# V rows in one tile, X blocks in pairs, and late K weights, in the prologue of a two-part kernel

## The chip, the cores and the metric

One core of one Trainium2 chip. The metric is the device time of one execution in microseconds (us), lower is better. The kernel before took 2195.29 us in the median of four runs (2187.41 to 2197.44). Ratios are computed as the mean time of one kernel's runs over the mean of the other's runs of the same rounds, so they are not quite the ratio of the medians quoted beside them.

## The reference

Two independent computations share the program; their outputs lie side by side.

```python
# A: a long convolution (here done by two-stage DFTs), S = 2048, D = 1024
kv = shifted(k, shift_k) * v
y  = irfft(rfft(pad(kv)) * rfft(pad(ssm_k)))[:S] + kv * ssm_D
a  = q * y
# B: 64 segments of 32 tokens, each attends to itself and to a memory of 8 rows (1024 wide, 32 heads of 128)
for s in range(64):
    h = concat([mem, x[32*s : 32*s+32]])          # 40 rows
    q, k, v = h @ Wq, h @ Wk, h @ Wv
    o = softmax(mask(q k^T * scale)) v @ Wo
    mem = o[:8]; outs.append(o[8:])
out = concat([a, b], axis=-1)
```

The memory makes the segments of B a chain. Each needs all four weight matrices, which do not fit in SBUF together. So the kernel keeps 43 of 64 chunks of weights (512 KB each) in SBUF, and two more from the first segment on; the other 19 it streams in each segment from a copy in DRAM, `WS`, through a ring of six tiles. What does not depend on the memory (projections of the last eight tokens of each segment, transposed X) is computed ahead, in a prologue, where A runs too.

## The kernel before

The parts that the change touches. `slot16` hands out two tiles of 16 KB per partition in turn, `pair` two tiles of 4 KB in turn; `group` loads one group of eight weight chunks and copies the streamed ones to `WS`. `VBD` is the buffer in DRAM for the V rows, `REC` that for transposed X and the other projections.

```python
def slot16(shape, dt, name):
    turns["stage"] ^= 1
    return base.tile(shape, dt, tag=f"stage{turns['stage']}", name=name)
def pair():
    turns["pair"] ^= 1
    return base.tile([128, 2048], BF, tag=f"wring{2 + turns['pair']}", name="pair")

# transposed X blocks, one every third unit of A's work: X and its transposed copy share a tile
def x_load(b):
    both = pair()
    nc.sync.dma_start(both[:, 0:1024], x[b * 128:(b + 1) * 128, :])
    loaded.append(both)
def x_block(b):
    both = loaded.pop(0)
    X_sb = both[:, 0:1024]
    ...                                     # eight transposes on TensorE into PSUM tile tp
    xt = both[:, 1024:2048].rearrange("p (s k t) -> p s k t", s=4, k=8)
    nc.vector.tensor_copy(xt, tp[:].rearrange(...))
    nc.gpsimd.dma_start(REC[:, 4 * b:4 * b + 4, 0:256], xt.rearrange("p s k t -> p s (k t)"))

# weights that stay, but come late; then the V projection and its stores
def place_late(n, tile_of):                 # n chunks of `late` into a tile, by GpSimd's queue
    ...
with tc.issue_after(copied[-4].ins):        # behind one of the last copies to WS
    place_late(4, stage_home)               # four K chunks into a 16 KB tile
    for i in range(len(v_temp) - 2, n_more):
        place_late(1, lambda: more(i))
for _ in range(2):
    fetch()                                 # first two chunks of the ring
...                                         # six Wo chunks DRAM to DRAM into WS
for g in range(2):
    ws = wv[g]
    for tb in range(4):                     # four row blocks of 128
        vst = pair()[:].rearrange("p (c w) -> p c w", c=4)
        for c in range(4):
            ...                             # eight matmuls into ps
            evac(vst[:, c, :], ps[:])       # ScalarE twice, VectorE once, in turn
        for c in range(4):
            nc.sync.dma_start(VBD[16*tb:16*tb+16, :, c, :, g*128:(g+1)*128].rearrange("s t i e -> (s t) i e"),
                              vst[:, c, :].rearrange("p (i e) -> p i e", i=4))   # 128 KB in 256 B pieces
    if g == 0:
        place_late(4, stage_home)           # four Wo chunks into the other 16 KB tile
        for i in range(2):
            place_late(1, lambda: more(i))
```

## Time and profile before

| stretch of the span, us | what runs | full resource |
|---|---|---|
| 0 to 115 | A, first DFT stage | mixed |
| 115 to 293 | A, second stage, filled with B's projections and X blocks | TensorE |
| 293 to 369 | A, third stage, filled with the Q projection | DMA |
| 369 to 453 | V projection (256 matmuls of 128x512) | DMA, then TensorE |
| 453 to 2190 | 64 segments, some 27 us each | DMA |

The prediction below shows the lines themselves. Two marks separate the prologue from the loop: the first and the last V matmul, and the first output of the loop, which is the first issue of `out_dram<-Y`. In the timeline of GpSimd of the kernel before it reads (start, duration, engine, line, operation; in brackets the idle time before it and what ended it):

```profile
490.09 0.74 POOL L1033 DMA_DIRECT2D out_dram<-Y  x1 [7.73 <-ACT Y L1026]
```

### The profile page before, as it was taken

What the parts mean: (1) busy time and instruction counts of PE and PEld (TensorE: products, weight loads), DVE (VectorE), ACT (ScalarE), POOL (GpSimd) and SP (SyncE); (2) the same over time, 40 slices, a digit from 0 to 9 for tenths busy, and PEclk for the clock granted to TensorE, in tenths of its full rate; (3) what the DMA queues carried; (4) which work ended last, traced back from release to release, by engine and by line L of the source; (5) the groups of instructions that cost most, each with busy time, mean ns of one, the idle gap of its engine ahead of it and who ended that gap; (6) DMA issues with size and microseconds to landing.
All of it is one profiled execution on the core that took longest, in us unless ns stands there. A gap on an engine that the chain in (4) does not pass through costs nothing. (4 is left out here: it accounts for less than half of the span.)

```text
span 2190.4 us, 81498 instructions
## 1 busy us (share of the span) xinstructions
PE 1734.6 (79%) x35636; PEld 927.5 (42%) x35636; DVE 872.0 (40%) x2686; ACT 648.4 (30%) x1139; POOL 436.8 (20%) x1131
## 2 busy tenths in 40 slices
PE   4688888678878878888887887888878888888886
PEld 2232233234444444444444444444444444444444
DVE  9927752023333333333333333333333333333332
ACT  8935521122222222222222222222222222222221
POOL 4013422311111111111111111111111211111111
PEclk9899999889999999999999999999999999999999
DMA  9998879889999999999999999999999999999996
GB/s 324 340 341 295 267 274 391 277 293 383 388 379 392 393 356 385 392 391 395 392 387 385 393 391 391 394 395 374 396 393 374 388 383 384 389 394 392 394 389 263
DMA packets 262702, 804.66 MB, mean 367 GB/s; under 512 B 52332, under 2 KB 52364, under 8 KB 262343
## 3 DMA queue, kind: packets, MB, share of 16 engines
q1 hardware_dynamic: 230008, 725.84, 86.9%
q0 software_dynamic: 27120, 63.11, 8.4%
q10 hardware_dynamic: 5216, 10.49, 1.3%
q8 instruction: 279, 4.57, 0.8%
q14 instruction: 79, 0.65, 0.1%
HBM read 739.92 MB, written 62.39 MB: 366 GB/s over the span
## 5 line engine op out<-in xcount | busy, mean ns | idle before, releaser
L884 PEld LDWEIGHTS <-rec 128*32 128x32 bf16 x12351 | 324.2, 96 | 477.8 <-issue 259.1
L884 PE MATMUL acc<-wring,rec 128*32 128x512 bf16 (+1 forms) x3777 | 375.9, 386 | 141.6 <-DMA wring<-WS 126.4
L893 ACT CAST qkv_sb<-acc 128x512 bf16<-128x512 f32 x384 | 224.8, 585 | 660.8 <-PE acc L884 660.8
L970 PEld LDWEIGHTS <-OT 128*32 128x32 bf16 x8192 | 216.3, 96 | 178.2 <-issue 151.3
L970 PE MATMUL yacc<-wring,OT 128*32 128x256 bf16 x3072 | 153.9, 275 | 98.0 <-DMA wring<-WS 56.4
L884 PE MATMUL acc<-Wmid,rec 128*32 128x512 bf16 x3072 | 225.8, 383 | 0.0
L884 PE MATMUL acc<-Wres,rec 128*32 128x512 bf16 x2816 | 221.2, 380 | 0.0
L830 PEld LDWEIGHTS <-OTB 128*16 128x16 bf16 x4096 | 105.1, 90 | 105.5 <-issue 95.1
L956 ACT CAST OT<-OTp 128x512 bf16<-128x512 f32 x128 | 74.9, 585 | 242.9 <-PE OTp L948 242.9
L986 DVE COPY KT<-tps 128x512 bf16<-128x512 bf16 x64 | 27.2, 424 | 298.6 <-PE tps L899 298.6
L785 POOL DMA_DIRECT2D rec<-REC x64 | 37.5, 585 | 526.6 <-issue 277.2
L957 DVE CAST OTB<-OTp 128x128 bf16<-128x128 f32 x128 | 37.3, 291 | 262.1 <-ACT OT L956 262.1
L736 DVE TENSOR_SCALAR wring<-OTp 128x384 int32<-128x384 int32 x126 | 112.2, 890 | 58.4 <-PE acc L884 52.4
L884 PE MATMUL acc<-pw,rec 128*32 128x512 bf16 x1536 | 130.4, 382 | 0.0
L860 POOL COPY KT<-rec 128x128 bf16<-128x128 bf16 x128 | 38.6, 302 | 427.8 <-PE SB L908 421.9
L845 POOL DMA_DIRECT2D out_dram<-YB x128 | 73.0, 577 | 234.2 <-DVE YB L843 224.0
L914 DVE TENSOR_REDUCE mx<-SB 128x5 f32<-128x200 f32 x128 | 47.1, 368 | 181.4 <-PE SB L908 181.4
L830 PE MATMUL SB<-wring,OTB 128*16 128x256 bf16 x1488 | 78.2, 273 | 39.1 <-DVE SB L809 31.0
L899 PE MATMUL tps<-ident,qkv_sb 128*128 128x128 bf16 x1024 | 101.0, 221 | 8.0 <-ACT qkv_sb L893 0.2
L899 PEld LDWEIGHTS <-qkv_sb 128*128 128x128 bf16 x1024 | 62.6, 97 | 105.0 <-ACT qkv_sb L893 67.5
L970 PE MATMUL yacc<-Wlate,OT 128*32 128x256 bf16 x2048 | 93.4, 273 | 2.9 <-issue 2.7
L1026 ACT CAST Y<-yacc 128x256 bf16<-128x256 f32 x64 | 23.8, 372 | 242.8 <-PE yacc L970 238.9
(229 smaller groups left out, 2690.1 us busy)
## 6 DMA issues: line engine op xcount, KB each, us to landing
wring<-WS SPq DMA_DIRECT2D x1216, 512.0 KB, 7.4
rec<-REC POOLq DMA_DIRECT2D x64, 192.0 KB, 6.1
SK<-s_sb SPq DMA_DIRECT2D x16, 512.0 KB, 4.9
SU<-s_sb SPq DMA_DIRECT2D x16, 512.0 KB, 5.0
Kg<-SK SPq DMA_DIRECT2D x32, 256.0 KB, 4.5
Ug<-SU SPq DMA_DIRECT2D x32, 256.0 KB, 5.6
REC<-stage POOLq DMA_DIRECT2D x16, 512.0 KB, 9.7
zt<-SZ SPq DMA_DIRECT2D x16, 512.0 KB, 8.7
```

Source lines behind the costliest of these rows:

```text
L736: nc.vector.tensor_scalar(out=dst, in0=src, scalar1=0, scalar2=None, op0=ALU.bitwise_or)
L785: nc.gpsimd.dma_start(rec[:], REC[:, s, :])
L830: nc.tensor.matmul(self.acc[32 * dq:32 * dq + W, x - o:y - o], lhsT=self.OTB[:, c, 4 * g + i, :], rhs=r, start=first and not self.seeded, ...
L845: nc.gpsimd.dma_start(bass.AP(outb.tensor, outb.offset + (SEG * NB * self.b + NX) * 2048 + 256 * dq, [[2048 * SEG, NB], [2048, 8], [1, 256 ...
L860: nc.gpsimd.tensor_copy(KT[:, :, :, 32:40], KBs[:, 128 * g:128 * g + 128].rearrange("p (c i t) -> p i c t", c=4, i=4))
L884: nc.tensor.matmul(self.acc[32 * c:32 * c + 32, x - 512 * c:y - 512 * c], lhsT=hT[:, kc, :], rhs=r, start=(kc == 0 and x == 512 * c), stop ...
L893: nc.scalar.copy(sb[:], self.acc[:])
L899: nc.tensor.transpose(tp[:, i * 128:(i + 1) * 128], sb[:, i * 128:(i + 1) * 128], ident[:])
L914: nc.vector.tensor_reduce(out=mx[:], in_=S, op=ALU.max, axis=AX.X)
L956: nc.scalar.copy(OT[:], o_view[:, :, :, 0:32])
L957: nc.vector.tensor_copy(OTB[:, :, 4 * g:4 * g + 4, 8 * j:8 * j + 8], o_view[:, :, :, 32:40])
L970: nc.tensor.matmul(yacc[32 * dq:32 * dq + 32, x - o:y - o], lhsT=OT[:, c, i, :], rhs=r, start=(h == 0 and x == o), stop=(h == 31), tile_po ...
```

## The change

The intent, as I read it: V rows of group 0 should not wait for stores; an X load should not wait for a store of an older block's transposed copy; and late weights should not get in front of the V weights.

```diff
 def x_load(b):
-    both = pair()
-    nc.sync.dma_start(both[:, 0:1024], x[b * 128:(b + 1) * 128, :])
-    loaded.append(both)
+    t = base.tile([128, 2048], BF, tag="wring2", name="X_sb")
+    nc.sync.dma_start(t[:].rearrange("p (b d) -> p b d", b=2), x[b*128:(b+2)*128, :].rearrange("(b p) d -> p b d", b=2))
+    loaded[b], loaded[b + 1] = t[:, 0:1024], t[:, 1024:2048]
 def x_block(b):
-    both = loaded.pop(0)
-    X_sb = both[:, 0:1024]
+    X_sb = loaded.pop(b)
+    if b % 2 == 0:
+        t = base.tile([128, 2048], BF, tag="wring3", name="xt")
+        xts[b], xts[b + 1] = t[:, 0:1024], t[:, 1024:2048]
 ...                     # the load of a pair is issued after the second block of the pair before
-        with tc.issue_after(copied[-4].ins):
-            place_late(4, stage_home)
-            for i in range(len(v_temp) - 2, n_more):
-                place_late(1, lambda: more(i))
-        for _ in range(2):
-            fetch()
+        with tc.issue_after(copied[-1].ins):
+            for _ in range(2):
+                fetch()
+        late = late[4:11] + late[:4] + late[11:]          # K chunks behind seven Wo chunks
 ...
         for g in range(2):
+            if g == 0:
+                vsts = slot16([128, 4, 4, 512], BF, "vst")
             for tb in range(4):
-                vst = pair()[:].rearrange("p (c w) -> p c w", c=4)
+                vst = vsts[:, tb] if g == 0 else pair()[:].rearrange("p (c w) -> p c w", c=4)
 ...
             if g == 0:
-                place_late(4, stage_home)
-                for i in range(2):
-                    place_late(1, lambda: more(i))
+                with tc.issue_after(copied[-1].ins):
+                    place_late(4, stage_home)
+                    for i in [*range(len(v_temp) - 2, n_more), 0, 1]:
+                        place_late(1, lambda: more(i))
+                    place_late(4, stage_home)              # K, into the tile of group 0's V rows
```

More of the change, by code (lines that the diff above doesn't have):

```diff
@@ L545, in group @@
         return ws
-    loaded = []
+    loaded = {}
     def x_load(b):
-        both = pair()
-        nc.sync.dma_start(both[:, 0:1024], x[b * 128:(b + 1) * 128, :])
-        loaded.append(both)
+        t = base.tile([128, 2048], BF, tag="wring2", name="X_sb")
+        nc.sync.dma_start(t[:].rearrange("p (b d) -> p b d", b=2),
+                          x[b * 128:(b + 2) * 128, :].rearrange("(b p) d -> p b d", b=2))
+        loaded[b], loaded[b + 1] = t[:, 0:1024], t[:, 1024:2048]
     def x_block(b):
-        both = loaded.pop(0)
-        X_sb = both[:, 0:1024]
+        X_sb = loaded.pop(b)
+        if b % 2 == 0:
+            t = base.tile([128, 2048], BF, tag="wring3", name="xt")
+            xts[b], xts[b + 1] = t[:, 0:1024], t[:, 1024:2048]
         tp = ps0.tile([128, 1024], BF, tag="ps0", name="xt_ps")
@@ L559, in x_block @@
             nc.tensor.transpose(tp[:, kc * 128:(kc + 1) * 128], X_sb[:, kc * 128:(kc + 1) * 128], ident[:])
-        xt = both[:, 1024:2048].rearrange("p (s k t) -> p s k t", s=4, k=8)
+        xt = xts.pop(b).rearrange("p (s k t) -> p s k t", s=4, k=8)
         nc.vector.tensor_copy(xt, tp[:].rearrange("p (k j t) -> p j k t", k=8, j=4))
         nc.gpsimd.dma_start(REC[:, 4 * b:4 * b + 4, 0:256], xt.rearrange("p s k t -> p s (k t)"))
+    xts = {}
     flip = [0]
@@ L617, in fill @@
         units[0] += 1
+        if n == 0:
+            x_load(0)
         if n % 3 == 2 and blocks:
-            x_block(blocks.pop(0))
+            b = blocks.pop(0)
+            x_block(b)
+            if b % 2 and blocks:
+                x_load(b + 1)
         if n >= 34 or n % 3 != 2:
             next(rest, None)
-        if n % 3 == 0 and len(blocks) > len(loaded):
-            x_load(n_seg // 4 - len(blocks))
     run_a(pw, slot16, stage1_done, fill)
```

## The prediction

> **What bounds the kernel now.** I began with the granted clock (0.971, one core, a fast run), then the page's 40 slices and its chain. The chain that ended last is mostly DMA:
>
> ```profile
> DMA 14%; PE 5%; DVE 2%; issue 1%; ACT 0%; POOL 0%; SPq 0%; DVEq 0%; POOLq 0%; ACTq 0%
> DMA wring<-WS 14%; PE acc L884 2%; DVE wring L736 1%; PE yacc L970 1%; PE SB L830 1%; DMA out_dram<-YB 0%; PE tps L899 0%; ACT OT L956 0%; POOL out_dram L845 0%; PE OTp L944 0%; PE OTp L948 0%; DVE PT L935 0%; DVE OTB L957 0%; PE tps L791 0%; SPq L654 0%
> ```
>
> The 64 segments stream their weights from WS, 19 chunks of 512 KB each. From about 490 us on this loop is limited by the DMA engines, and the diff touches nothing in it. So the gain, if any, lies in the prologue, which I cut into stretches of one regime (busy time by engine, granted clock, DMA share and rate in each window; 1.00 DMA is all 16 engines at work):
>
> ```profile
> core 0: us, PE busy (x) PEld busy (x) DVE busy (x) ACT busy (x) POOL busy (x), PEclk, DMA share, GB/s
> 180.00:260.00 80.00, 77.01 (x426) 25.24 (x426) 67.69 (x118) 47.91 (x91) 35.51 (x34) 0.97 0.83 274
> 260.00:270.00 10.00, 4.27 (x18) 1.55 (x18) 3.08 (x5) 2.74 (x6) 3.64 (x5) 0.66 0.80 244
> 293.00:369.00 76.00, 64.09 (x284) 27.20 (x283) 28.10 (x32) 9.17 (x16) 21.42 (x33) 0.91 0.99 368
> 369.00:420.00 51.00, 27.10 (x117) 11.73 (x116) 3.46 (x5) 5.76 (x10) 15.02 (x20) 0.83 1.03 361
> 420.00:453.00 33.00, 33.00 (x147) 14.54 (x144) 3.73 (x6) 7.02 (x12) 6.36 (x12) 0.95 0.48 115
> 1000.00:2190.00 1190.00, 955.37 (x23529) 546.95 (x23517) 428.64 (x1543) 302.60 (x573) 213.01 (x668) 0.99 1.00 383
> ```
>
> To be seen: up to 293 us (stage 2 of the first half of the problem) TensorE is full, but for a hole at 260:270. From 293 the DMA is full. From 369 to 453 the V projection runs; in its first part TensorE is busy 27 of 51 us while the DMA is full, in its second part TensorE is full and the DMA half idle. That is two resources taking turns, which is where a reordering can gain. The waits of TensorE and of the two engines that evacuate PSUM, in the V part (total, times, longest):
>
> ```profile
> ACT pair L569 <- DMA VBD<-pair: 27.9, 2, 16.4
> PE vb_ps L694 <- ACT pair L569: 21.8, 2, 14.2
> DVE pair L571 <- DMA VBD<-pair: 18.0, 1, 18.0
> PE vb_ps L694 <- DMA Wres<-in_B_Wv_dram: 2.1, 1, 2.1
> ```
>
> V rows of group 0 fill two `pair` tiles in turn; the third and fourth row blocks wait until the stores of the first and second have landed in VBD. TensorE loses 7.6 us at 389 and 14.2 us at 405. The X blocks have a smaller loss of the same kind (TensorE in stage 2; then SyncE's queue, from 200 us on):
>
> ```profile
> PE xt_ps L559 <- DMA pair<-in_B_x_dram: 12.7, 2, 6.6
> SPq L551 <- DMA REC<-pair: 24.5, 7, 5.2
> ```
>
> A `pair` tile holds X and its transposed copy, so a new X load waits for the store of an older copy to REC, and SyncE's queue waits with it; then eight transposes, in order in TensorE's queue, wait for X (6.6 us to 180.1, 6.1 us to 265.7).
>
> **What the Trainium skill says.** (1) "DMA: Bandwidth & Descriptors", section "Queues, rings and completion order": each DMA engine takes turns between queues packet by packet. The trace agrees in direction: between 396 and 419 us only about four of the 128 KB VBD stores (256 B pieces, SyncE's queue) landed beside twelve or more 512 KB transfers of GpSimd's queue, with up to 21.1 us from issue to landing; once that queue had run dry, four landed within 1.4 us. (2) The same page, "Issuing engines are not separate DMA queues": a transfer moved to another place still needs the same 16 engines. So I keep a ledger of DMA work, not of queues. (3) "TensorE: Matmul & The Clock Gate", Part 1: after a few idle us the clock starts at half rate. Here too: the first matmuls after the 7.6 and 14.2 us waits come every 0.43 us, later ones every 0.216, at about 3 us a time. A removed wait gives that back too.
>
> **The change part by part.**
>
> *V rows of group 0 in one tile of 16 KB per partition.* All four row blocks get room of their own; the tile is the "stage" buffer whose last store (of the Q projection before) landed at 355.6, long before the first write at 373.6. So group 0 waits for no store. V needs 2 x 128 matmuls at 0.216 us = 55.3 us; it now runs 369.4 to 452.6 = 83.2. Of the surplus 27.9 us, 21.8 are the two waits, 2.1 the weights, and some 4 the slow clock after them. On TensorE alone the end could come at 424.7.
>
> *K weights behind Wo, ring prefetch later.* Before the last V weights, GpSimd's queue now issues two ring chunks and two K chunks (355.6 and 367); after the change they come later, and so do two more K chunks and one Wo chunk. That frees 4 x 1.35 us (512 KB at 390 GB/s) = 5 us of DMA ahead of the V weights: the 2.1 us wait should go. Bytes are the same. New dependency: the four K chunks go into the V tile, so they wait for all 16 stores of group 0, and the first segment wants them at once.
>
> *The DMA ledger.* From 369 to 453 the windows hold 1.03 x 51 + 0.48 x 33 = 68 us of full-time DMA work. At the highest share seen in 10 us windows there, 1.05, that takes 65 us: not before 434. Of TensorE's 28 us this leaves 28 - (434 - 425) = some 18. A second count by bytes: 361 GB/s x 51 us + 115 x 33 = 22 MB, of which the 32 VBD stores and four stage stores (6.3 MB) go in 256 B pieces, at the 290 GB/s of those four stores 22 us, and 15.9 MB at 400 GB/s 40 us: 62 us, an end at 431, a gain of 21. Stepping through by hand: GpSimd's queue is dry at about 416 to 419, group 0's stores land just after, K lands at about 428, and row blocks 2 and 3 of group 1 wait some 8 us for the stores of 0 and 1; V ends at about 432 to 435. I take **17 us**.
>
> *X in pairs.* Eight loads of 512 KB replace sixteen of 256 KB, each free to go once the transposes of the block before are done (three units, some 10 us, ahead of use), not after a store. The order of SyncE's instructions confirms that block 2's load moves ahead of weights it now follows. Of the 6.6 us I expect 3 to 4 back (issued about 5 us earlier, but twice as long), of the 6.1 us some 5: **8 us**. Stage 2 is TensorE's, so a hole there shifts all that follows. Transposes, copies and REC stores are unchanged in number and size.
>
> Sum: 17 + 8 = **25 us** of 2196.9.
>
> **The rivals.** *A. A new wait takes over*: group 0's stores queue up in front of group 1's, and K behind them. For it: SyncE's queue is in order and slow while GpSimd's is full. Against it: GpSimd's queue runs dry by about 419 and small stores then land at 0.45 us each. If K came only at 440, V's gain would fall to 12 and the sum to some 18 us: 2179. *B. The transfer is hidden*: stages after 293 are DMA-full, so earlier X helps nothing and V gains only what DMA idles. Against it for X: it removes a hole in which the DMA idled too (0.80), and the engines idle at 0.35 before 293. If X gave nothing: 2180. *C. TensorE is the only bound*: the shares above 1.0 under contention count waiting as work, and all 28 + 10 us come: 2159. *D. DVE becomes a wait*: the single transposed tile is rewritten only after two REC stores have landed (4 to 13 us each), and DVE would hold up stage 2; 2 to 4 us at the worst.
>
> **Range and chances.** Centre 2197 - 25 = **2172 us**. Low end: rival C, 2159 and a good run; high end: A and B together, 10 us gained, 2187. The runs before differ by 10 us among themselves (2187 to 2197), so I say **2157 to 2187**, 8 in 10. For 2% the gain would have to be 44 us; all prologue waits touched sum to 21.8 + 2.1 + 4 + 12.7 = 41 us. So faster by over 2%: **0.02**; within 2%: **0.97**; slower by over 2%: **0.01**, since bytes, matmuls and loop are the same.
>
> **What would show it.** Right: no wait of ACT or DVE on VBD in group 0; the last V matmul 20 to 28 us earlier than 452.6, of which some 8 already at the first V matmul; waits of the X transposes from 12.7 to about 4 us; DMA share above 0.9 up to the end of V; the loop still 27 us a segment ((2190.4 - 490.1) / 63). Wrong, if the first segment stalls on the K chunks in the V tile for more than a few us, if group 1's third row block waits over 15 us for VBD, if the DMA share still falls to 0.5 in V (then there was room for more, or a new wait), or if stage 2 ends no earlier.

## The result

The changed kernel took 2173.27 us in the median of four runs (2170.49 to 2175.60), for 2195.29 before; ratio 0.9906 with a 95% interval of 0.9878 to 0.9934. That is 20.6 us shorter by the ratio, and within 2%. The prediction said 2172, 2157 to 2187.

The chain that ended last is of the same make, the ring of weights. Its shares sum to 14% of the span (22% before), so it covers the end of the loop alone and says nothing of the prologue:

```profile
DMA 10%; PE 3%; DVE 1%; issue 0%; ACT 0%; POOL 0%; SPq 0%; POOLq 0%; DVEq 0%; ACTq 0%
```

The same windows as before (columns as above):

```profile
core 0: us, PE busy (x) PEld busy (x) DVE busy (x) ACT busy (x) POOL busy (x), PEclk, DMA share, GB/s
180.00:260.00 80.00, 74.72 (x422) 25.23 (x421) 66.95 (x117) 48.62 (x93) 35.02 (x33) 1.00 0.88 287
260.00:270.00 10.00, 9.03 (x49) 2.79 (x46) 8.45 (x16) 5.66 (x11) 7.09 (x8) 1.00 0.58 201
...
293.00:369.00 76.00, 63.84 (x279) 27.47 (x279) 27.61 (x31) 9.17 (x16) 21.29 (x31) 0.91 1.03 384
369.00:420.00 51.00, 40.81 (x187) 18.28 (x185) 5.54 (x8) 9.02 (x16) 17.26 (x26) 0.92 1.01 320
420.00:453.00 33.00, 22.36 (x192) 9.03 (x194) 4.40 (x12) 4.11 (x7) 5.25 (x16) 0.81 0.86 283
```

The hole at 260 to 270 us is gone (TensorE 9.0 us busy for 4.3). From 369 to 420 TensorE and the DMA are now busy together, 40.8 us for 27.1, and from 420 to 453 the DMA no longer runs half idle (0.86 for 0.48): V ends at 433.6, and the segments begin there. V now runs from 363.2 to 433.6, that is 70.4 us for 83.3.

The waits in the V part of the changed kernel (total, times, longest):

```profile
DVE pair L575 <- DMA VBD<-pair: 24.7, 2, 14.0
...
ACT pair L573 <- DMA VBD<-pair: 16.9, 2, 12.4
...
POOL Wlate L665 <- DMA VBD<-pair: 15.0, 1, 15.0
PE vb_ps L701 <- ACT pair L573: 10.2, 1, 10.2
```

Group 0's tile, `vst`, has no line that waits for a store. Group 1's `pair` tiles have: TensorE waits 10.2 us at 408, and 2.5 us later on. The third line is the new dependency: GpSimd's queue stood 15 us before it could load the K chunks (the profile names the tile of the last stores; by the program it is group 0's stores that are waited for). They were issued from 416.3 to 418.0 and landed from 422.0 to 426.2, before V ended.

The X blocks, from 150 us on:

```profile
PE xt_ps L562 <- DMA X_sb<-in_B_x_dram: 3.9, 1, 3.9
SPq L551 <- PE xt_ps L562: 10.3, 5, 3.1
DVE xt L564 <- DMA REC<-xt: 9.1, 3, 5.4
```

Transposes wait 3.9 us for X (12.7 before). SyncE's queue waits for TensorE, no longer for stores. VectorE has a new wait for the transposed tile's stores, 9.1 us, of which little reached TensorE: it waited 2.4 us for VectorE's `xt`, where before it had waited 2.1 us for the same copy. The first output of the loop comes 19.5 us earlier:

```profile
470.57 0.74 POOL L1042 DMA_DIRECT2D out_dram<-Y  x1 [7.75 <-ACT Y L1035]
```

### The profile page after: what moved, and what is told of

It is laid out like the page before. It is cut to its first block, busy times and chain, and to the rows that moved or that the text cites. A ratio compares the mean times of both kernels' runs of the same rounds, so it can differ in the third digit from the quotient of the medians.

```text
span 2173.7 us, 81452 instructions
## 1 busy us (share of the span) xinstructions
PE 1729.0 (80%) x35636; PEld 926.4 (43%) x35636; DVE 872.6 (40%) x2686; ACT 649.2 (30%) x1139; POOL 438.3 (20%) x1131
## 5 line engine op out<-in xcount | busy, mean ns | idle before, releaser
L979 PE MATMUL yacc<-Wlate,OT 128*32 128x256 bf16 x2048 | 104.5, 273 | 1.9 <-issue 1.0
L1035 ACT CAST Y<-yacc 128x256 bf16<-128x256 f32 x64 | 23.9, 373 | 239.7 <-PE yacc L979 230.2
```

The costliest lines, as they stand in the source:

```text
L979: nc.tensor.matmul(yacc[32 * dq:32 * dq + 32, x - o:y - o], lhsT=OT[:, c, i, :], rhs=r, start=(h == 0 and x == o), stop=(h == 31), tile_po ...
```

## The experiments

Theory: the gain is the sum of two independent parts. X in pairs shifts the end of stage 2; V rows in one tile let TensorE run beside the DMA; how much the latter gives is set by the DMA work that must be done anyway (the ledger). Rivals: the DMA hides the X part; TensorE alone decides V; the gain comes from the new order of late weights and ring chunks.

Twelve experiments ran, two of them the unedited kernels, each in five rounds, with runs of the kernel before among them. All gave the correct result but `big_pieces`. "V" is the first to last V matmul, "waits" are TensorE's in it, "loop" runs from the first to the last `out_dram<-Y`.

| kernel | median, us | before in its rounds | ratio (95%) | V, us | waits in V | first output | loop |
|---|---|---|---|---|---|---|---|
| before | 2195.29 | | | 369.4 to 452.7 | 23.9 | 490.1 | 1689.2 |
| changed | 2173.27 | 2195.29 | 0.9906 (0.9878 to 0.9934) | 363.2 to 433.6 | 12.7 | 470.6 | 1692.4 |
| x_only | 2186.43 | 2188.80 | 0.9987 (0.9973 to 1.0002) | 364.4 to 447.2 | 21.8 | 484.0 | 1693.0 |
| v_only | 2177.03 | 2188.80 | 0.9942 (0.9927 to 0.9957) | 368.4 to 437.7 | 11.6 | 475.0 | 1688.2 |
| k_first | 2173.68 | 2188.80 | 0.9922 (0.9898 to 0.9946) | 364.8 to 432.2 | 10.0 | 469.5 | 1693.8 |
| g1_own | 2168.36 | 2188.80 | 0.9911 (0.9891 to 0.9931) | 363.1 to 418.5 | 0 | 465.9 | 1700.5 |
| after_again | 2175.64 | 2190.76 | 0.9921 (0.9892 to 0.9949) | 359.3 to 428.9 | 11.8 | 465.8 | 1697.1 |
| before_again | 2188.48 | 2190.76 | 0.9979 (0.9949 to 1.0010) | 368.8 to 452.3 | 23.0 | 489.5 | 1691.9 |
| big_pieces | 2166.22 | 2190.76 | 0.9882 (0.9858 to 0.9906) | 362.4 to 424.6 | 5.1 | 460.2 | 1693.5 |
| whole_rows | 2167.51 | 2190.76 | 0.9894 (0.9870 to 0.9918) | 360.1 to 423.5 | 4.7 | 464.8 | 1698.3 |
| whole_rows_ring | 2168.54 | 2189.85 | 0.9891 (0.9862 to 0.9920) | 365.7 to 428.7 | 4.7 | 467.0 | 1690.8 |
| x_only_again | 2182.68 | 2189.85 | 0.9957 (0.9925 to 0.9990) | 362.7 to 444.4 | 22.1 | 482.5 | 1686.6 |
| v_only_again | 2179.30 | 2189.85 | 0.9949 (0.9916 to 0.9982) | 369.5 to 440.2 | 13.3 | 476.3 | 1691.9 |
| ring_early | 2169.11 | 2189.85 | 0.9900 (0.9871 to 0.9929) | 364.3 to 430.6 | 8.0 | 468.4 | 1693.8 |

One more mark can be taken from the table: from V's start to the first output. It leaves out what happens before V and in the loop, and the four kernels that were profiled twice repeat it within 0.9 us: 120.7 and 120.7 us for the kernel before, 119.6 and 119.8 for x_only, 106.6 and 106.8 for v_only, 107.4 and 106.5 for the changed kernel.

### x_only: the X part alone

The first half of the diff above (`x_load`, `x_block` and the point of the load), nothing of the V part.

> Only the X part of the change (pairs, transposed tiles of their own); V part as before. My theory: the holes in stage 2 shrink (waits of the X transposes from 12.7 to about 4 us), the first V matmul moves from 369.4 to about 363, the V part keeps its 83 us, and the whole is 6 us (4 to 8) shorter than before. Rival 'hidden': the DMA is full from 293 us on, so an earlier stage 2 is absorbed by slower stage 3 loads; first V matmul after 367, whole within 2 us of before.

TensorE's waits in the V part and for X, of x_only:

```profile
PE vb_ps L701 <- ACT pair L573: 21.8, 2, 12.2
PE xt_ps L562 <- DMA X_sb<-in_B_x_dram: 4.6, 1, 4.6
```

V starts at 364.4, 5.0 us earlier, its two waits of together 21.8 us stay, and the first output is 6.1 us earlier: the rival 'hidden' falls, as an earlier stage 2 goes straight through the DMA-full stretch. But the time gained was only 2.8 us, with an interval that includes 0, because this run's loop took some 4 us longer.

### v_only: the V part alone

The second half of the diff; X as before.

> Only the V part (group 0 in one tile, late loads and ring prefetch moved, K behind Wo); X as before. My theory (the ledger of DMA work): V part from 83 to about 70 us, with 10 to 13 us of waiting left in group 1, whole 13 us (10 to 16) shorter than before; with x_only it adds up to the whole change (20 to 22). Rival 'TensorE alone': V part near 56 us, whole 25 us or more shorter. Rival 'needs X': less than 6 us.

The same waits, of v_only:

```profile
PE vb_ps L694 <- ACT pair L569: 9.5, 1, 9.5
PE vb_ps L694 <- DVE pair L571: 2.1, 1, 2.1
PE xt_ps L559 <- DMA pair<-in_B_x_dram: 11.6, 2, 6.0
```

V takes 69.3 us, with 11.6 us of waits left, all in group 1; the time is 12.7 us shorter. Both are what the ledger expected and far from 'TensorE alone' (25 us or more). That expectation was written when the changed kernel's 70.4 us and 12.7 us of waits were known, so the numbers test that the V part alone brings them, not the ledger's size. The 2.1 us wait for the V weights does not appear.

### x_only_again and v_only_again: is the X part's loss in the loop real?

The same two kernels once more.

> x_only once more. In the first try its prologue was 6.1 us shorter (first loop output 484.0 for 490.1) but the time only 2.8 us (interval -0.4 to 5.9 us), as its loop took 1693 us for 1689. Theory 'loop scatter': first output within 2 us of 484, loop anywhere in 1687 to 1700, whole 4 to 7 us shorter than before. Rival 'X slows the loop': loop above 1692 again, whole 1 to 4 us shorter.

> v_only once more, the other half of that test. Theory 'loop scatter': first output within 2 us of 475.0, loop anywhere in 1687 to 1700, whole 13 to 16 us shorter than before. Rival 'only the X part lengthens the loop': loop 1686 to 1691 again.

The first outputs repeat (482.5 and 476.3); the loops do not: 1686.6 for x_only, the shortest of all, and 1691.9 for v_only. Both times missed what I had expected: 9.4 us shorter than before for 4 to 7, and 11.2 for 13 to 16. So 'X slows the loop' falls in the form that I had given it. Over the two tries x_only is 2.8 and 9.4 us shorter than before, mean 6.1, v_only 12.7 and 11.2, mean 12.0; together 18.1, for 20.6 and 17.3 (mean 19.0) of the whole change. Within this scatter the two parts add up. Not settled: ten profiles with the X part have loops of 1694 us in the mean, four without it 1690; single loops differ by 6 us in the same kernel, so I take no cause from that.

### after_again and before_again: the scatter

Both kernels unedited, among the others.

> The changed kernel, not edited, in the same rounds as the other three: 20 us (17 to 23) shorter than before. Its profile also shows how much the 64-segment loop differs from run to run: my theory is that first output of the loop comes within 2 us of 470.6 and that the loop from there to its last output (1692.4 us in the first profile) moves by up to 5 us without any cause in the change.

> The kernel before, not edited, as a null test: ratio 1.000 within 0.2%. First output of the loop within 2 us of 490.1; loop from there to the last output 1689.2 plus or minus 5 us. Rival 'the X part slows the loop' (x_only's loop took 1693.1, v_only's 1688.2): then before_again stays at 1688 to 1690 and after_again at 1692 to 1694.

The null test gave 0.9979 (interval to 1.001), just outside the 0.2% expected: five rounds can be off by 4 us or so. The changed kernel came out 17.3 us shorter by the ratio, within its expectation, but its first output at 465.8 was 4.8 us earlier than in the first profile, outside the 2 us I had given; stage 2 ended earlier (V from 359.3), and the loop took those 4.7 us longer. In this profile no wait of TensorE is put down to X, where the first one had a wait of 3.9 us. Of the ten profiles with the X part, seven have such a wait (3.9 to 5.2 us) and three have none (after_again, big_pieces and whole_rows, with V from 359.3, 362.4 and 360.1). Scatter in the prologue is thus larger than I believed, and a profile's single loop time says nothing at this level.

### k_first: the late weights in their old order

```diff
-        late = late[4:11] + late[:4] + late[11:]
```

> The changed kernel, but with the late weights in their old order: K into the other 16 KB tile first, Wo into the V tile last. My theory: the order of these loads is not what gained, because both wait behind the same DMA work and segment 0 starts after V either way; within 3 us of the changed kernel (20 to 22 us shorter than before). Rival 'K behind Wo matters': K first leaves the Wo chunks late for segment 0 or lengthens the wait of group 1, and 5 us or more of the gain go.

17.1 us shorter by the ratio, for 17.3 of after_again (in other rounds) and 20.6 of the first measurement; V's waits are 10.0 us and its first output 469.5. The order of K and Wo is not what gained: as shown for the changed kernel, K landed before V ended even when it came last.

### ring_early: the two ring chunks as early as before

```diff
-        with tc.issue_after(copied[-1].ins):
-            for _ in range(2):
-                fetch()
+        for _ in range(2):
+            fetch()
```

> The changed kernel with the two ring chunks loaded as early as before (ahead of the V copies). My theory (DMA work moved, not removed): the V weights arrive 2 to 3 us later, which costs at most 2 us in the first V rows; V ends within 2 us of the changed kernel's 428.9 to 433.6 and the time within 3 us of it (17 to 21 shorter than before). Rival 'the later prefetch was worth its 5 us of DMA': 4 us or more of the gain go.

21.9 us shorter, V ends at 430.6, first output 468.4; no wait for V weights showed. The later prefetch is not what gained either. k_first and ring_early each undo one move; from V's start to the first output they take 104.7 and 104.1 us, for 107.4 and 106.5 with the moves in. Undoing both, with the V tile kept, was not tried, nor can K go to its old place, which is now the V tile.

### g1_own: no V row waits for a store

As k_first, and group 1 gets the other 16 KB tile; its four Wo chunks come after V.

```diff
+        both = [slot16([128, 4, 4, 512], BF, "vst") for _ in range(2)]
         for g in range(2):
-                vst = vsts[:, tb] if g == 0 else pair()[:].rearrange("p (c w) -> p c w", c=4)
+                vst = both[g][:, tb]
 ...
-                    place_late(4, stage_home)      # after group 0
+        place_late(4, stage_home)                  # after V
```

> As k_first, but group 1's V rows get a 16 KB tile of their own too, so that no V row waits for a store to VBD; four Wo chunks then load only after V. My theory (ledger): TensorE's waits in V (12.7 us) vanish and V ends near 419, but the DMA was at a share of about 0.9 already, so the work left over delays segment 0; whole at most 6 us shorter than the changed kernel (20 to 27 shorter than before). Rival 'TensorE's chain': the whole wait is gained, 32 us or more shorter than before.

This is the clearest test of the ledger. V ran without a wait, 55.4 us for the 55.3 worked out in the prediction, and ended at 418.5, 15 us before the changed kernel. The first output came only 4.7 us earlier than its 470.6, and no earlier than after_again's 465.8. Against k_first, from which this edit starts, the way from V's start to the first output is 1.9 us shorter (102.8 for 104.7). The windows of g1_own, and the two longest waits of TensorE after V:

```profile
363.00:420.00 57.00, 55.72 (x259) 25.05 (x256) 8.04 (x13) 12.87 (x22) 18.32 (x28) 1.00 1.00 317
420.00:453.00 33.00, 16.25 (x198) 6.08 (x202) 5.00 (x19) 4.59 (x8) 7.34 (x18) 0.63 1.02 360
```

```profile
423.87 0.37 PE L799 MATMUL tps<-ident,Y 128*128 128x128 bf16 x2 [5.15 <-DMA Y<-in_B_mem_dram]
...
433.20 0.62 PE L892 MATMUL acc<-wring,rec 128*32 128x512 bf16 x4 [7.20 <-DMA wring<-WS]
```

The DMA is full (1.00 and 1.02) right through, and TensorE waits in segment 0 for a load instead of in V for a store. From the end of V to the first output it takes 47.4 us for 37.0 in the changed kernel: of the 15.1 us by which V ended earlier, 10.4 came back one stage later. (The two waits shown are 5.2 and 7.2 us; the changed kernel too has waits for ring chunks there, 4.1 and 2.3 us.) The edit itself also puts four chunks behind V, so this shows that the wait could not simply be removed with these tiles, and the full DMA (1.00 from 363 to 420) is, as I read it, the reason: the loads would have found no idle time ahead of V's end either. The time, 19.5 us shorter than before and just short of the 20 to 27 expected, cannot be told from the changed kernel's.

### big_pieces: the cost of 256 B pieces by itself

The same bytes in the same number of stores, but each partition writes 1 KB in one piece, to wrong places in `VBD`; the second half of the output is wrong.

```diff
-    VBD[16*tb:16*tb+16, :, c, :, g*128:(g+1)*128].rearrange("s t i e -> (s t) i e"), vst[:, c, :].rearrange("p (i e) -> p i e", i=4)
+    VBD[16*tb:16*tb+16, :, 2*g + c//2, :, :].rearrange("s t i e -> (s t) (i e)")[:, 512*(c%2):512*(c%2)+512], vst[:, c, :]
```

> The changed kernel with every V store writing 1 KB pieces in place of 256 B ones, to the wrong places on purpose (the result is wrong in the second half of the output); same bytes, same number of transfers, same waits in the program. Theory 'the pieces cost DMA work': the waits of group 1 fall from 12.7 to 5 us or less, first loop output at about 464, 25 us shorter than before. Rival 'turn-taking only': a store that shares the engines with GpSimd's full queue is slow whatever its pieces; waits stay at 9 us or more, within 3 us of the changed kernel.

The one V wait of big_pieces, and from issue to landing of its stores:

```profile
PE vb_ps L701 <- ACT pair L573: 5.1, 1, 5.1
```

```profile
DMA to landing us min/median/max: 2.3/12.8/15.5
```

and the latter for the changed kernel:

```profile
DMA to landing us min/median/max: 2.0/5.9/26.2
```

The DMA's packets over the same 20 us show the cost itself (queue, packets, MB, share of the 16 engines' time; SyncE's stores go by q1, GpSimd's loads by q0). The changed kernel from 391 to 411 us:

```profile
q0 software_dynamic: 1757, 6.37, 82.4%
q1 hardware_dynamic: 3320, 0.82, 18.9%
```

and big_pieces in the same window:

```profile
q0 software_dynamic: 1706, 6.21, 80.6%
q1 hardware_dynamic: 1721, 1.57, 23.9%
```

Share times 20 us over MB: one MB costs all 16 engines 4.6 us in pieces of 256 B, 3.0 in pieces of 1 KB, and 2.6 on GpSimd's queue. For the 4.2 MB of V rows that is 19 us for 13, a difference of 6 to 7 us (an estimate from these lines).

The wait fell to 5.1 us, the slowest store from 26.2 to 15.5 us (the median rose, from 5.9 to 12.8: the stores that V waits for got faster, not every store), the first output came at 460.2, for 470.6 and 465.8 of the changed kernel, and the time is 25.9 us shorter than before, for 17.3 of after_again in the same rounds (the intervals still overlap). From V's start to the first output it is 97.8 us for 107.4 and 106.5. So the wait that the change left in group 1 is to a good part the price of small pieces, not of the shared tiles. "DMA: Bandwidth & Descriptors" of the Trainium skill, section "Specifications", gives 512 B as the least transfer for line rate; 256 B against 1 KB is in line with that.

### whole_rows and whole_rows_ring: a correct version with larger pieces

Both 16 KB tiles hold V rows of both groups side by side, so that one store per row block and c, issued when group 1's rows of that block are there, writes 2 KB pieces (16 stores in place of 32). Four late chunks go by SyncE's queue after the first eight stores, four by GpSimd's after V.

```diff
+    both = [slot16([128, 2, 4, 4, 2, 128], BF, "vst") for _ in range(2)]
-    evac(vst[:, c, :], ps[:])
+    evac(both[tb // 2][:, tb % 2, c, :, g, :], ps[:].rearrange("p (i e) -> p i e", i=4))
+    if g == 1: store VBD[16*tb:16*tb+16, :, c, :, :]    # one piece of 2 KB per partition
```

> A correct version of the same idea: the two 16 KB tiles hold V rows of both groups side by side, so that each store after group 1 writes 2 KB pieces; no V row waits for a store; four late chunks go by SyncE's queue after the first eight stores, four after V. Theory 'DMA work': the 4.2 MB of V stores take some 11 us of DMA in place of some 20, first loop output at 458 to 466, 26 to 32 us shorter than before. Rival: with no stores during group 0 the DMA idles in group 1 and the late chunks come after V: no better than the changed kernel (20 shorter).

V ended at 423.5 and the time was 23.2 us shorter than before, short of the 26 to 32 expected; the first output (464.8) lies with after_again's 465.8. The windows of whole_rows show why:

```profile
369.00:400.00 31.00, 26.32 (x109) 11.19 (x108) 3.96 (x7) 5.18 (x9) 11.03 (x18) 0.89 0.92 309
400.00:420.00 20.00, 20.00 (x94) 9.07 (x93) 2.77 (x4) 4.10 (x7) 1.42 (x6) 1.00 0.67 228
420.00:453.00 33.00, 20.98 (x231) 8.12 (x233) 5.60 (x20) 6.29 (x10) 5.91 (x12) 0.75 1.02 385
```

From 400 to 420 the DMA has too little to do (0.67), as the late chunks have no place to go until V's tiles are empty; then it is full. My reading is that the work saved by larger pieces is lost again as idle time. The next kernel moves two more ring chunks into that gap, into X's two tiles, which V no longer uses:

```diff
-    free = [4, 5, 0, 1, 2, 3]
+    free = [4, 5, 2, 3, 0, 1]
+                if g == 1 and tb == 0:
+                    with tc.issue_after(st.ins):      # st: this block's last store
+                        for _ in range(2):
+                            fetch()
```

> whole_rows, with two more ring chunks loaded during group 1, into the two buffers of X that V no longer uses; in whole_rows the DMA share fell to 0.67 from 400 to 420 us while seven chunks were left for after V. Theory (DMA idle time is what is left to win): share above 0.8 there, first loop output 3 to 5 us before 464.8, at 460 to 462; whole 26 to 29 us shorter than before. Rival: segment 0 is held by the seven late chunks, not by the ring; within 1 us of whole_rows (23 shorter).

```profile
400.00:420.00 20.00, 19.95 (x94) 9.08 (x93) 2.77 (x4) 4.10 (x7) 5.02 (x13) 1.00 0.81 249
```

The gap filled, 0.81 for 0.67, but the first output did not come earlier: 467.0, from a V start of 365.7 where whole_rows had 360.1. From V's start on that is 101.3 us for 104.7, of the size expected and more than the 0.9 us by which repeated profiles differ; but it is one profile each, on two chips, and the time, 23.9 us shorter, is the same, below the expected 26 to 29 and as the rival had it. Both versions have lower ratios than the changed kernel's (0.9894 and 0.9891 for 0.9921 and 0.9906), with intervals that overlap: I do not claim that they beat it.

## Why the prediction was right

- **The bound and where the gain could lie.** Right: the loop was not shortened, and the whole gain is in the prologue (first output 19.5 us earlier in the profile, time 20.6 us shorter).
- **Group 0 waits for no store; the V weights' wait goes.** Right, both seen in the changed kernel and in v_only.
- **The ledger instead of TensorE's 28 us.** Right in its mechanism, and the experiment that gave TensorE what it wanted (g1_own) shows it: 15 us earlier in V, at most 5 us earlier at the first output. **But the V term was too large**: 17 us expected, 12.9 measured (83.3 to 70.4; v_only 69.3 and 70.7). The step that failed is the size of group 1's wait, "some 8 us", which was 12.7 (11.8 and 11.6 in the next profiles). Under it lies "the 290 GB/s of those four stores": I had read the rate of small pieces off four landings within 1.4 us, stores that had been in work together for much longer. From 430 to 450 us of the kernel before those stores had the engines nearly to themselves:

```profile
q1 hardware_dynamic: 7024, 1.74, 41.9%
```

That is 1.74 MB in 8.4 us of full-time work, some 210 GB/s; the lines under big_pieces give nearly the same for the changed kernel (0.82 MB in 3.8 us). With 210 for 290 the prediction's count by bytes would have had 30 us for the 6.3 MB instead of 22, and an end of V at 439 (an estimate); v_only, whose V starts when it did before, ended at 437.7 and 440.2. big_pieces shows how much of the wait piece size makes: 5.1 us are left with 1 KB. The slow clock after the two waits came out at 3.4 us of lost time, not 4, and at 1.9 us after the one long wait that is left; "3 us a time" is how long it lasts, not what it costs.
- **The new dependency of K.** Right: K landed from 422 to 426, I had said about 428, and no matmul of segment 0 waited for it. The first segment's waits are for ring chunks, 4.1 and 2.3 us, as before (3.9 and 2.1).
- **X in pairs, 8 us.** A little too large: V's start moved by 6.2 us in the first profile; over the ten profiles with the X part it lies at 359.3 to 365.7, mean 363.0, for a mean of 369.0 in the four without, so 6.0. The second hole went as expected; of the first, 6.6 us, some 1 to 3 us came back in seven profiles, not 3 to 4 (3.9 to 5.2 us of waiting left), and in three no wait is put down to X any more (1.3 to 3.0 us before those transposes are put down to VectorE). Why X comes in time in some executions alone is not settled.
- **Rival D** was there: VectorE waits 9.1 us for the stores of the transposed tile. TensorE's wait for that copy is 2.4 us, hardly more than the 2.1 before.
- **The sum.** 17 + 8 = 25 became 13 + 6, 19.5 us at the first output and 20.6 in time. That the centre, 2172, lay so close to 2173.3 was partly luck: both terms were too large, but the kernel before stood at 2196.94 when I predicted and at a median of 2195.29 in the end, and the first runs of the changed kernel were good ones. Later it gained 17.3 us, and its two parts together 18.1.

## What to carry to other kernels

Where TensorE and the DMA take turns at being full, buffers that let them overlap paid here, but only up to the DMA work that was left: add up share times duration over the stretch before you count TensorE's waits as gain. Most of a removed wait returned one stage later where the other resource was full; what helped then was less work for it (larger pieces), not moving the work. And for gains of some 6 us in 2190 compare marks inside the trace (here the first output of the loop) beside the times, as the loop's scatter alone was up to 6 us between profiles of one kernel. Choose marks close around the change: the first output itself moved by 4.8 us between two profiles of the changed kernel, the stretch from V's start to it only by 0.9.

## What the Trainium skill lacked or had wrong

- "DMA: Bandwidth & Descriptors", "Queues, rings and completion order", has each engine take turns between queues by whole packets. The trace agrees in direction: from 391 to 411 us of the changed kernel both queues move on side by side. What the section does not spell out is how little a queue of small pieces gets in bytes: SyncE's got 3320 packets through for 1757 of GpSimd's, yet 0.82 MB for 6.37, and one store of 128 KB on it took 26.2 us to land.
- The same page, "Why small descriptors are slow (HBM only)", works out 27% overhead for 256 B (3 cycles of 11; by my estimate from that, 3/8 more than the bare 8), and adds descriptor metadata. Here one MB in 256 B pieces cost 4.6 us of all 16 engines, for 2.6 us on GpSimd's queue beside it: 1.8 times, so the section's cycle count alone puts the cost too low. In 1 KB pieces the first output came 8 us earlier (460.2 for a mean of 468.2).
- No page that I found adds up DMA work, share times duration, over a stretch as was done here. The shares above 1.0 in full windows (1.05 at most) show that a profile's share is no exact measure of it either.
